# A fused MLP forward and backward on one core: the first pair in half-height products, w1's left-over rows loaded in three pieces, two early pairs in q's banks, all four orders rewritten

## The chip, the cores and the metric

The kernel runs on one core of a Trainium2 chip. The engines are TensorE (PE, with PEld for its weight loads), VectorE (DVE), ScalarE (ACT), GpSimd (POOL) and SyncE (SP, which here only issues transfers). The metric is the time of one execution on the device in microseconds. The kernel before takes 266.25 us, the median of three runs (266.03 to 266.30); the execution that was profiled took 265.99 us, of which the profile covers a span of 264.2 us.

## The reference

A two-layer MLP with GELU, and all its gradients. S is 2048 rows, D is 448, F is 1792, everything is bf16.

```
def _fwd_reference(x, w1, b1, w2, b2):
    h = jnp.einsum("bsd,df->bsf", x, w1) + b1
    h = _gelu(h)                                  # tanh form
    return jnp.einsum("bsf,fd->bsd", h, w2) + b2

_out, _vjp = jax.vjp(_f, x, w1, b1, w2, b2)
return (_out, *_vjp(grad_out))                    # out, gx, gw1, gb1, gw2, gb2
```

## The kernel before, in words

**Tiling.** The 2048 rows are four blocks b of 512. The 1792 columns of F are 14 tiles of 128, taken as 7 pairs per block, so there are 28 pairs p (p = 7b + pair). For each pair the kernel computes u = x w1 (512 rows by two tiles), q = grad_out w2^T, h = gelu(u) and gh = q gelu'(u). From h comes out (units `o`), from gh comes gx (units `x`). At the end, over all rows, come gw1 (line 755) and gw2 (line 809), each 224 or more products of full height.

**Half-height products.** D is 448 = 3 x 128 + 64 rows of contraction. `uq_run` (line 245) cuts all of it into pieces of 64 rows and lets two products of 64 rows run side by side, one on the upper and one on the lower half of the array. One u or q of a pair is a run `.1` of three such double slots, which starts both banks, and a run `.2` of four, which ends them; seven slots of 512 columns. Between the two runs the halves change banks. `run` (line 224) therefore puts a GpSimd instruction between them (`nc.gpsimd.nop`, line 233) when nothing else guarantees that the first run has ended: TensorE's first product of the second run waits for GpSimd, and GpSimd for the end of the first run. In the orders another run nearly always stands in between.

Run `.2` reads a second copy of w1's first 64 rows, on partitions 64 to 127, shifted by one column (`w1f` pieces of the load; "repeated rows"); both runs read w1's last 64 rows ("left-over rows", `w1r`). Before the change the very first pair is computed otherwise: in two halves of 256 columns (tokens `h0`, `h1`), each by `full_run` (line 275), with products of 128 rows for k = 0 to 2 and of 64 rows for k = 3.

**Orders.** Nothing is scheduled by a tool. `Plan` holds one list of operations per engine, in the order of the strings PE_ORDER, ACT_ORDER, DVE_ORDER and SP_ORDER (lines 91 to 132); each engine's queue is strictly in order, and semaphores between engines follow from who writes and reads what. The tokens that matter:

- PE: `h0.1` is half 0 of pair 0, run 1 (before the change `h0.0` is all of half 0); `u5.2` and `q5.2` are run 2 of pair 5; `p1.0` to `p1.3` are the out units of pair 1 of block 0, two slots each; `o1.0.4.9.1` and `x...` are out and gx units (block, half of the rows, first and last tile, run).
- ACT and DVE: `c5A`, `c5B` copy u out of its two banks with the bias; `s`, `g`, `t` are Square, GELU and Tanh on ACT; `e r y z m n` are the derivative's steps on DVE; `G5` multiplies by q and frees q's banks.
- SP: `L0` to `L4` are parts of w1's first 384 rows, `R` its left-over rows and (before) `R2`, `R3` the repeated rows; `K0` to `K3` parts of w2; `X1`, `Y0` transposed blocks of x and grad_out; `J0` to `J3` parts of w2 transposed, `I0`, `I1` halves of w1 transposed, `E` four small copies (`ends`); then `So`, `Sx` stores, `H` stores of h, `T` transposes of gh.

q of pairs 0, 1, 2 and 3, and 4 to 6 of each block need J0, J1, J2 and J3 (`W2_PART`, line 306); `p` units of the same pairs need K0 to K3.

**Banks.** PSUM has eight banks. q lives in banks 6 and 7; u in 4 and 5, but for the pairs in `U_BANK` (line 134); the out and gx units in 0 to 3.

**Semaphores of transfers.** The transfers of SP and ACT share eight semaphores in turn; the order listing shows each transfer waiting for the one eight before it.

Of the kernel before, what the change touches and what calls it, by code (L numbers as in the profile page):

```python
# [96 lines left out]
x0.1.0.6.1 q9.1 u16.1 q9.2 u16.2 x0.0.0.6.2 q10.1 u17.1 q10.2 u17.2 x0.1.0.6.2 q11.1 x0.0.6.10.1 u18.1 q11.2 u18.2
x0.1.6.10.1 x0.0.6.10.2 x0.1.6.10.2 u19.1 q12.1 u19.2 q12.2 x0.0.10.14.1 u20.1 x0.1.10.14.1 u20.2 x0.0.10.14.2
x0.1.10.14.2 q13.1 o2.0.0.6.1 q13.2 o2.1.0.6.1 o2.0.0.6.2 o2.1.0.6.2 q14.1 o2.0.6.10.1 q14.2 o2.1.6.10.1 o2.0.6.10.2
q15.1 u21.1 q15.2 u21.2 o2.1.6.10.2 o2.0.10.14.1 o2.1.10.14.1 u22.1 q16.1 u22.2 q16.2 o2.0.10.14.2 u23.1 o2.1.10.14.2  # L100
u23.2 q17.1 x1.0.0.6.1 x1.1.0.6.1 q17.2 x1.0.0.6.2 x1.1.0.6.2 x1.0.6.10.1 x1.1.6.10.1 q18.1 x1.0.6.10.2 u24.1 q18.2
# [17 lines left out]
c7B r3 y3 z3 G1 m3 e4 n3 r4 y4 z4 G2 e5 r5 m4 z5 vo0.2 vo0.3 vo0.0 vo0.1 G3 y5 n4 e6 r6 y6 z6 G4 m5 e7 n5 r7 y7 m6 z7
G5 n6 e8 r8 m7 z8 y8 n7 G6 e9 r9 y9 z9 m8 n8 m9 G7 vo1.0 vo1.1 vo1.2 vo1.3 n9 e10 r10 y10 z10 G8 m10 e11 n10 r11 y11  # L120
z11 G9 m11 e12 n11 r12 y12 z12 G10 m12 e13 n12 r13 y13 z13 G11 m13 e14 n13 r14 y14 z14 m14 n14 G12 e15 r15 y15 z15
vx0.0 vx0.2 G13 m15 e16 n15 r16 y16 z16 m16 G14 n16 e17 r17 y17 z17 G15 m17 e18 n17 r18 y18 z18 m18 n18 G16 vo2.0
vo2.1 vo2.2 vo2.3 e19 r19 y19 z19 m19 G17 n19 e20 r20 y20 z20 m20 n20 G18 e21 r21 y21 z21 vx1.0 G19 e22 vx1.3 m21 r22
# [35 lines left out]
def make_plan(tc, ctx, x, w1, b1, w2, b2, grad_out, out_0, out_1, out_2, out_3, out_4, out_5):  # L159
    nc = tc.nc  # L160
    P = 128
# [113 lines left out]
    def full_run(w, t, banks, pair, c0, c1):  # L275

        two = []
        for i in (0, 1):
            ft = 2 * (pair % NPB) + i
            for k in range(4):  # L280
                rows = slice(0, 128) if k < 3 else slice(0, 64)
                two.append((k == 3, i, k, lambda i=i, k=k, ft=ft, rows=rows: nc.tensor.matmul(  # L282
                    bk_(banks[i])[:, 0:c1 - c0], lhsT=w[rows, k, ft * P:(ft + 1) * P], rhs=t[rows, k, EDGE + c0:EDGE + c1],
                    start=(k == 0), stop=(k == 3), skip_group_check=True)))
        for _, _, _, product in sorted(two, key=lambda m: m[:3]):
            product()

# [111 lines left out]
    def C(p, h, eng, hf=None):  # L399
        ft = 2 * (p % NPB) + h  # L400
        v = val(("ub", p), F_UB[p])
        if hf is None:
# [4 lines left out]
        bias = b1T[:, ft:ft + 1]
        if eng == "ACT":
            fn = lambda: nc.scalar.activation(out=out, in_=src, func=ACT.Identity, bias=bias)  # L409
# [177 lines left out]
    def LW1R(part, eng="SP"):  # L587

        c0, c1 = ((0, 1024), (1024, F))[part % 2]
        if part < 2:  # L590
            dma(eng, f"w1r{part}", w1_sb[0:64, 3, c0:c1], w1[MAIN:D, c0:c1], [], [("w1r", part)], (c1 - c0) * 128)
        else:
            dma(eng, f"w1f{part - 2}", w1_sb[64:128, 3, c0:c1], w1[0:64, c0:c1], [], [("w1f", part - 2)], (c1 - c0) * 128)
# [259 lines left out]
```

## Time and profile before

| | |
|---|---|
| median of three runs | 266.25 us (266.03 to 266.30) |
| profiled execution | 265.99 us, span 264.2 us |
| PE busy | 260.4 us, 99% of the span |
| DVE, ACT, POOL busy | 198.9, 130.6, 14.1 us |
| forward and gradient units (line 238) | from 7.5 us to 176.6 us |
| gw1 (line 755), gw2 (line 809) | 42.5 us each, to the end |
| mean DMA traffic | 175 GB/s |

An engine's busy time counts from the start of an instruction to its modelled end; PE's products overlap, so its 99% means that there is always one under way, not that the array is full. In a timeline each row is a start, a length, the engine, the source line, the operation with the tiles that it writes and reads, the number of instructions that were merged into the row, and in brackets the idle time before it with what ended it. SPq rows are transfers being issued: their length is the time that SP spends on the issue, not that of the transfer.

### The profile page before, as it was taken

Reading aid. Unit: us, or ns where it says so; the run is one execution under the profiler, and the core shown is the slowest. Engines: PE = TensorE matmul, PEld = TensorE weight load, DVE = VectorE, ACT = ScalarE, POOL = GpSimd, SP = SyncE. Lnnn points to the kernel's source line nnn. Section 1 sums busy time; section 2 is a strip of 40 time slices with the busy share of each in tenths; the row PEclk is TensorE's granted clock in tenths of the full one; section 3 lists DMA queues with packets and bytes.
Section 4 is the critical chain, followed back from the end, with each engine's and each line's share of the span. In section 5 each row is a group of like instructions: output and inputs, shape, how many; then the busy total and the mean of one; then the engine's idle time right before and its main releaser. Section 6 shows DMA issues by size and latency. Waiting matters only on the chain.

```text
span 264.2 us, 5339 instructions
## 1 busy us (share of the span) xinstructions
PE 260.4 (99%) x2170; PEld 182.7 (69%) x2170; DVE 198.9 (75%) x289; ACT 130.6 (49%) x168; POOL 14.1 (5%) x8
## 2 busy tenths in 40 slices
PE   8999999999999999999999999999999999999995
PEld 4488988888888886677777777765555555555554
DVE  6887998999998789897876998339999999311000
ACT  4899786996998936736696511011112111000001
POOL 0000000000000000000000000000000393400000
PEclk9999999999999999999999999999999999999999
DMA  7999689999999953393665934794799988984221
GB/s 199 278 189 257 118 174 189 333 243 257 229 219 197 231 139 66 87 223 85 74 173 160 291 99 104 132 309 108 164 228 158 168 218 171 244 157 130 69 72 35
DMA packets 120235, 46.10 MB, mean 175 GB/s; under 512 B 96671, under 2 KB 120081, under 8 KB 120210
## 3 DMA queue, kind: packets, MB, share of 16 engines
q1 hardware_dynamic: 119636, 45.43, 76.6%
q8 instruction: 17, 0.28, 0.4%
q10 hardware_dynamic: 574, 0.33, 0.4%
q14 instruction: 8, 0.07, 0.1%
HBM read 7.70 MB, written 14.28 MB: 83 GB/s over the span
## 4 chain that ended last, share of the span: by engine, by line
PE 97%; ACT 1%; DVE 1%; issue 0%; ACTq 0%; DVEq 0%
PE bank L238 46%; PE bank L755 16%; PE bank L809 16%; PE qb L238 16%; PE qb L365 1%; ACT TR L427 1%; PE bank L282 1%; PE bank L564 1%; DVE ub L411 0%; ACT ub L409 0%; DVE TR L432 0%; DVE TR L437 0%; PE qb L630 0%; ACT w_sb L814 0%; ACTq L427 0%
## 5 line engine op out<-in xcount | busy, mean ns | idle before, releaser
L238 PEld LDWEIGHTS <-HG 64*128 64x128 bf16 x896 | 70.9, 94 | 17.8 <-issue 0.7
L238 PE MATMUL qb<-gT,w2Tf 64*128 64x512 bf16 x392 | 55.9, 376 | 0.0
L238 PE MATMUL bank<-xT,w1f 64*128 64x512 bf16 x378 | 53.4, 376 | 0.0
L238 PE MATMUL bank<-w_sb,HG 64*128 64x448 bf16 x448 | 51.2, 349 | 0.4 <-ACT ub L409 0.4
L238 PE MATMUL bank<-w1T_sb,HG 64*128 64x448 bf16 x448 | 48.4, 349 | 0.0
L809 PE MATMUL bank<-w2Tf,HG 128*128 128x448 bf16 (+2 forms) x240 | 42.6, 340 | 0.0
L755 PE MATMUL bank<-w1f,gh_nat 128*128 128x448 bf16 x224 | 42.5, 352 | 0.0
L467 DVE SCALAR_TENSOR_TENSOR HG<-TR,qb 128x1024 bf16<-128x1024 bf16 x28 | 34.1, 1217 | 9.6 <-PE qb L238 9.4
L238 PEld LDWEIGHTS <-w2Tf 64*128 64x128 bf16 x392 | 32.6, 94 | 8.2 <-issue 0.2
L238 PEld LDWEIGHTS <-w1f 64*128 64x128 bf16 x378 | 31.4, 94 | 8.3 <-issue 0.3
L809 PEld LDWEIGHTS <-HG 128*128 128x128 bf16 x240 | 22.9, 98 | 19.8
L755 PEld LDWEIGHTS <-gh_nat 128*128 128x128 bf16 x224 | 21.8, 98 | 20.6 <-issue 0.4
L452 ACT ACTIVATE TR<-TR 128x1024 bf16<-128x1024 bf16 x28 | 29.3, 1050 | 11.3 <-DVE TR L442 11.3
L778 DVE TENSOR_TENSOR w1T_sb<-w1T_sb,gh_nat 128x1792 f32<-128x1792 f32 x14 | 28.4, 2025 | 0.5
L457 DVE TENSOR_SCALAR TR<-TR 128x2048 bf16<-128x2048 bf16 x28 | 19.3, 689 | 8.3 <-ACT TR L452 8.3
L760 ACT ACTIVATE TR<-bank 128x448 bf16<-128x448 f32 x14 | 7.6, 543 | 34.9 <-PE bank L755 34.9
L815 DVE CAST w_sb<-bank 128x448 bf16<-128x448 f32 x6 | 3.7, 624 | 25.9 <-PE bank L809 25.9
L814 ACT CAST w_sb<-bank 128x448 bf16<-128x448 f32 (+2 forms) x9 | 4.4, 490 | 37.7 <-PE bank L809 37.7
L784 POOL PARTITION_ALL_REDUCE w1T_sb<-w1T_sb x1 | 10.7, 10662 | 208.3 <-DVE w1T_sb L782 208.3
L409 ACT ACTIVATE ub<-bank,b1T 128x512 bf16<-128x512 f32 (+1 forms) x26 | 16.2, 666 | 10.9 <-DVE TR L442 6.0
L462 DVE TENSOR_TENSOR TR<-TR 128x1024 bf16<-128x1024 bf16 x28 | 19.2, 686 | 0.2
L447 DVE TENSOR_TENSOR TR<-TR,HG 128x1024 bf16<-128x1024 bf16 x28 | 19.2, 684 | 0.0
(45 smaller groups left out, 183.6 us busy)
## 6 DMA issues: line engine op xcount, KB each, us to landing
hT_dram<-HG SPq DMA_DIRECT2D x28, 256.0 KB, 3.4
out_dram<-st SPq DMA_DIRECT2D x16, 224.0 KB, 2.7
w1f<-in_x_dram SPq DMA_DIRECT2D x2, 896.0 KB
w2Tf<-in_grad_out_dram SPq DMA_DIRECT2D x2, 560.0 KB
out_dram<-w_sb SPq DMA_DIRECT2D x2, 448.0 KB, 2.7
out_dram<-xT SPq DMA_DIRECT2D x2, 384.0 KB, 3.1
w_sb<-in_w_dram SPq DMA_DIRECT2D x1, 672.0 KB
w2Tf<-in_grad_out_dram SPq DMA_DIRECT2D x1, 672.0 KB, 4.6
```

The costliest lines, as they stand in the source:

```text
L238: m = nc.tensor.matmul(bk_(b)[:, 0:n], lhsT=l, rhs=r, start=st, stop=sp, skip_group_check=True)
L409: fn = lambda: nc.scalar.activation(out=out, in_=src, func=ACT.Identity, bias=bias)
L447: pl.op("DVE", f"R{p}", lambda: nc.vector.tensor_tensor(out=t[:, 1], in0=t[:, 1], in1=hblk(p), op=ALU.mult), [("r", p), ("h", p)], [val((" ...
L452: pl.op("ACT", f"t{p}", lambda: nc.scalar.activation(out=t[:, 0], in_=t[:, 0], func=ACT.Tanh), [("y", p)], [val(("t", p), ("TR0", p % NTR) ...
L457: pl.op("DVE", f"m{p}", lambda: nc.vector.tensor_scalar(out=t[:], in0=t[:], scalar1=1.0, scalar2=None, op0=ALU.subtract), [("t", p), ("r2" ...
L462: pl.op("DVE", f"n{p}", lambda: nc.vector.tensor_tensor(out=t[:, 0], in0=t[:, 0], in1=t[:, 1], op=ALU.mult), [("m0", p), ("m1", p)], [val( ...
L467: pl.op("DVE", f"G{p}", lambda: nc.vector.scalar_tensor_tensor(out=ghblk(p), in0=t[:, 0], scalar=2.0, in1=qb[:, :, :], op0=ALU.subtract, o ...
L755: nc.tensor.matmul(bk_(bk)[:, 0:D], lhsT=gh_nat[:, st // 4, ft, st % 4, :], rhs=x_nat[:, st, :], start=(st == 0), stop=(st == NS - 1))
L760: fn = (lambda dst=dst, src=src: nc.scalar.mul(out=dst, in_=src, mul=-0.5)) if eng == "ACT" else \
L778: nc.vector.tensor_tensor(out=hs3, in0=a, in1=gh_nat[:, st // 4, :, st % 4, :], op=ALU.add)
L784: pl.op("POOL", "gb1", lambda: nc.gpsimd.partition_all_reduce(gb1_w, hsum, channels=P, reduce_op=bass_isa.ReduceOp.add), ["hsc"], ["gb1"], ...
L809: nc.tensor.matmul(bk_(bk)[:, 0:d1 - d0], lhsT=h_nat[ft][:, st, :], rhs=g_nat[:, st, d0:d1], start=(st == 0), stop=(st == NS - 1))
```

## The change

1. `full_run` is gone. Pair 0's halves are two runs each like every other pair: `h0.1 h0.2 h1.1 ... h1.2`, seven double slots of 256 columns per half.
2. Since `h0.2` needs the repeated rows and the shifted column of x at once, w1's left-over and repeated rows are each loaded in three parts (columns 0 to 256, 256 to 1024, 1024 to 1792) instead of two, six small loads instead of four; the copy of x's edge column (`Dx0`) waits for one quarter of the block only.
3. Pairs 2 and 5 keep u in banks 6 and 7 (before, pair 2 had banks 2 and 3 and pair 5 had 4 and 5). More buffers for u's copies are used (`UB` up to 13).
4. All four orders are new. Out and gx units are cut at tiles 4 and 9 instead of 6 and 10.

On TensorE, where pair 0 begins, there stand before (w1f is w1, xT0 the transposed first block of x):

```order
L282 MATMUL bank4_93<-xT0_68,w1f_64 128x256
L282 LDWEIGHTS w1f_64
L282 MATMUL bank5_94<-xT0_68,w1f_64 128x256
L282 LDWEIGHTS w1f_64
L282 MATMUL bank5_94<-xT0_68,w1f_64 128x256
L282 LDWEIGHTS w1f_64
L282 MATMUL bank5_94<-xT0_68,w1f_64 128x256
L282 LDWEIGHTS w1f_64
L282 MATMUL bank4_93<-xT0_68,w1f_64 128x256
```

and after, at the seam of `h0.1` and `h0.2` (rows of 64 partitions each, two side by side):

```order
L238 MATMUL bank5_94<-xT0_68,w1f_64 128x256
L238 LDWEIGHTS w1f_64
L238 MATMUL bank4_93<-xT0_68,w1f_64 128x256
L238 LDWEIGHTS w1f_64
L238 MATMUL bank4_93<-xT0_68,w1f_64 128x256
L238 LDWEIGHTS w1f_64
L238 MATMUL bank5_94<-xT0_68,w1f_64 128x256
```

The third of these products is the first of `h0.2`; it follows `h0.1` directly and waits for GpSimd.

On SP, the first loads after x's rows, before (64x1024 and 64x768 are left-over and repeated rows, 128x3x256 are L1, L2, L3, 128x3x768 is L4, w2_sb are K0, K1, K2):

```order
L507 DMA w1f_64<-in_w1_dram 64x1024
L507 DMA w1f_64<-in_w1_dram 128x3x256
L507 DMA w1f_64<-in_w1_dram 64x1024
L507 DMA w1f_64<-in_w1_dram 128x3x256 x2
L507 DMA w1f_64<-in_w1_dram 64x768
L507 DMA w2_sb_66<-in_w2_dram 128x2x448
L507 DMA w1f_64<-in_w1_dram 128x3x768
L507 DMA w2_sb_66<-in_w2_dram 128x2x448
L507 DMA w1f_64<-in_w1_dram 64x768
L507 DMA w2_sb_66<-in_w2_dram 128x4x448
```

and after:

```order
L499 DMA w1f_64<-in_w1_dram 64x256 x2
L499 DMA w1f_64<-in_w1_dram 128x3x256
L499 DMA w1f_64<-in_w1_dram 64x768 x3
L499 DMA w1f_64<-in_w1_dram 128x3x256 x2
L499 DMA w2_sb_66<-in_w2_dram 128x2x448
L499 DMA w1f_64<-in_w1_dram 128x3x768
L499 DMA w1f_64<-in_w1_dram 64x768
L499 DMA w2_sb_66<-in_w2_dram 128x6x448
L499 DMA w2_sb_66<-in_w2_dram 128x4x448
L499 DMA w2_sb_66<-in_w2_dram 128x2x448
```

L2 has moved from the fourth to the seventh place, and K3 (6x448) has come forward into this list, ahead of K2 and K1.

On SP, the transposes that follow, before (w2Tf in the order J0, J1, J2, J3 with the tail of J3 from `ends`; w1T_sb are I0 and I1, gT1 is Y1):

```order
L519 DMA_TRANSPOSE gT0_70<-in_grad_out_dram 128x4x512
L519 DMA_TRANSPOSE xT1_69<-in_x_dram 128x4x544
L519 DMA_TRANSPOSE w2Tf_65<-in_w2_dram 128x4x256
L507 DMA w2_sb_66<-in_w2_dram 128x6x448
L519 DMA_TRANSPOSE w2Tf_65<-in_w2_dram 128x4x256
L519 DMA_TRANSPOSE w2Tf_65<-in_w2_dram 128x4x512
L507 DMA ends_72<-in_x_dram 16x448
L507 DMA ends_72<-in_grad_out_dram 16x448
L507 DMA ends_72<-in_w2_dram 16x448 x2
L519 DMA_TRANSPOSE w2Tf_65<-in_w2_dram 128x4x752
L521 DMA_TRANSPOSE w2Tf_65<-ends_72 128x4x16
L510 DMA_TRANSPOSE w1T_sb_67<-in_w1_dram 128x7x448 x2
```

and after:

```order
L511 DMA_TRANSPOSE xT1_69<-in_x_dram 128x4x544
L511 DMA_TRANSPOSE gT0_70<-in_grad_out_dram 128x4x512
L511 DMA_TRANSPOSE w2Tf_65<-in_w2_dram 128x4x256
L511 DMA_TRANSPOSE w2Tf_65<-in_w2_dram 128x4x512
L511 DMA_TRANSPOSE w2Tf_65<-in_w2_dram 128x4x256
L502 DMA_TRANSPOSE w1T_sb_67<-in_w1_dram 128x7x448
L511 DMA_TRANSPOSE gT1_71<-in_grad_out_dram 128x4x544
L502 DMA_TRANSPOSE w1T_sb_67<-in_w1_dram 128x7x448
L499 DMA ends_72<-in_x_dram 16x448
L499 DMA ends_72<-in_grad_out_dram 16x448
L499 DMA ends_72<-in_w2_dram 16x448 x2
L511 DMA_TRANSPOSE w2Tf_65<-in_w2_dram 128x4x752
```

I0, Y1 and I1 now stand ahead of `E` and J3 (the 752 columns).

The diff, with a line or two of each order:

```diff
 PE_ORDER = """
-W7 X0 X1 X2 X3 B h0.0 h1.0 u1.1 u2.1 u1.2 u3.1 u2.2 u3.2 p0.0 p0.1 u4.1 p0.2 p0.3 u4.2 p1.0 p1.1 p1.2 u5.1 p1.3 p2.0
+W7 X0 X1 X2 X3 B h0.1 h0.2 h1.1 u1.1 h1.2 u2.1 u1.2 u3.1 u2.2 u3.2 p0.0 p0.1 p0.2 p0.3 u4.1 u5.1 u4.2 u5.2 p1.0 p1.1
...
-u8.2 q2.1 p5.2 p5.3 q2.2 u9.1 p6.0 p6.1 u9.2 q3.1 p6.2 p6.3 q3.2 u10.1 o1.1.0.6.1 u10.2 q4.1 o1.0.0.6.1 u11.1 q4.2
+p5.0 p5.1 q1.2 u9.1 p5.2 p5.3 u9.2 q2.1 p6.0 p6.1 q2.2 u10.1 p6.2 p6.3 u10.2 q3.1 o1.1.0.4.1 q3.2 u11.1 o1.0.0.4.1
+u11.2 q4.1 o1.0.0.4.2 q4.2 u12.1 o1.1.0.4.2 u12.2 q5.1 o1.0.4.9.1 u13.1 q5.2 u13.2 o1.1.4.9.1 o1.0.4.9.2 q6.1
...
 SP_ORDER = """
-xr12 xr24 R0 L1 R2 L2 L3 R1 K0 L4 K1 R3 K2 Y0 X1 J0 K3 J1 J2 E J3 I0 I1 Y1 X2 So0.1 H0 H1 H2 H3 H4 H5 H6 H7 H8 T0 T1
+xr12 xr24 R0 F0 L1 R1 F1 R2 L2 L3 K0 L4 F2 K3 K2 K1 X1 Y0 J0 J2 J1 I0 Y1 I1 E J3 X2 So0.1 So0.0 H0 H1 H2 H3 H4 H5 H6
...
-UB = (0, 1, 2, 3, 4, 5, 6, 7, 8, 9, 0, 1, 2, 3, 4, 5, 6, 7, 8, 9, 0, 1, 2, 0, 1, 2, 0, 1)
-U_BANK = {1: 0, 2: 2}
+UB = (0, 1, 2, 3, 4, 5, 6, 7, 8, 9, 10, 11, 12, 13, 0, 1, 2, 3, 4, 5, 6, 0, 1, 2, 0, 1, 2, 0)
+U_BANK = {1: 0, 2: 6, 5: 6}
...
-    def full_run(w, t, banks, pair, c0, c1):
...
+    REST = (0, 1, 1, 1, 2, 2, 2)
+    REST_COLS = ((0, 256), (256, 1024), (1024, F))
...
-        rd = [part_w1(p), ("w1r", int(p % NPB > 3))] + [("xT", b, h) for h in hs]
-        if d == 0:
-            pe(f"u{p}.{d}{tag}", lambda: full_run(w1_sb, xT[b % 2], bk, p, *c), rd, vs, ("s256", 8), (None, 0))
-            return
+        rd = [part_w1(p), ("w1r", REST[p % NPB])] + [("xT", b, h) for h in hs]
         if d == 2:
-            rd += [("xe", b), ("w1f", int(p % NPB > 3))]
+            rd += [("xe", b), ("w1f", REST[p % NPB])]
...
-              [(tag, 0, 0)], [v], ("tiny", 1))
+              [(tag, 0, 0) if tag == "gT" else "row0"], [v], ("tiny", 1))
...
+    def LW1F(part, eng="SP"):
+
+        c0, c1 = REST_COLS[part]
+        dma(eng, f"w1f{part}", w1_sb[64:128, 3, c0:c1], w1[0:64, c0:c1], [], [("w1f", part)], (c1 - c0) * 128)
```

More of the change, by code (lines that the diff above doesn't have):

```diff
@@ L97 @@
[L97 to L101, printed above, removed]
@@ L119 @@
[L119 to L123, printed above, removed]
@@ L124 @@
-y22 z22 n21 G20 m22 e23 n22 r23 y23 z23 m23 n23 G21 e24 r24 y24 z24 m24 G22 n24 e25 vx2.2 r25 vx2.3 z25 y25 G23 m25
-e26 n25 r26 y26 z26 m26 G24 n26 e27 r27 y27 z27 G25 m27 vo3.0 vo3.1 n27 vo3.2 vo3.3 G26 G27 vx3.1 vx3.3
+ident X0 Dx0 X2 b1T b2c c0B0 c0B1 c1B e0 r0 y0 c2B c3B z0 e1 r1 y1 z1 c4B e2 c5B r2 y2 z2 c6B m0 n0 Dg0 c7B m1 n1 G0 m2 e3
+n2 r3 y3 z3 G1 e4 r4 m3 z4 n3 y4 G2 vo0.2 vo0.3 m4 vo0.0 vo0.1 n4 G3 e5 e6 r5 r6 z5 z6 y5 y6 G4 m5 m6 n5 n6 e7 r7 y7
+z7 G5 e8 r8 y8 z8 m7 n7 G6 m8 e9 n8 r9 y9 vo1.0 vo1.1 z9 vo1.2 m9 vo1.3 n9 G7 e10 r10 y10 z10 m10 G8 n10 e11 r11 y11
@@ L273, in unit_run @@
         run(slots)
-    def full_run(w, t, banks, pair, c0, c1):
[L277 to L286, printed above, removed]
     def gap(bank):
@@ L411, in C, with after @@
             fn = lambda: nc.vector.tensor_scalar(out=out, in0=src, scalar1=bias, scalar2=None, op0=ALU.add)
-        pl.op(eng, f"c{p}{'AB'[h]}{'' if hf is None else hf}", fn, [uv, "b1T"], [v], ("copy", 512 if hf is None else 256))
+        o = pl.op(eng, f"c{p}{'AB'[h]}{'' if hf is None else hf}", fn, [uv, "b1T"], [v], ("copy", 512 if hf is None else 256))
+        if hf is None and u_banks(p)[0] == 6 and eng == "ACT" and f"c{p}B" in DVE_ORDER.split():
+            after(o, [("u", p, 1)])
+    def after(o, vs):
+        o["after"] = vs
+        return o
     def hblk(p):
@@ L571, in XC @@
         fn = (lambda: nc.scalar.copy(out=out, in_=src)) if eng == "ACT" else (lambda: nc.vector.tensor_copy(out=out, in_=src))
-        pl.op(eng, f"xc{t}", fn, [("xt", t)], [val(("xT", 0, t // 2), ("xT", 0, t // 2))], ("copy", 512))
+        pl.op(eng, f"xc{t}", fn, [("xt", t)], [val(("xT", 0, t // 2), ("xT", 0, t // 2))] + (["row0"] if t == 0 else []), ("copy", 512))
     def LX(src, dst, tag, b, hs):
@@ L587, in LW1R @@
     def LW1R(part, eng="SP"):
[L589 to L593, printed above, removed]
+        c0, c1 = REST_COLS[part]
+        dma(eng, f"w1r{part}", w1_sb[0:64, 3, c0:c1], w1[MAIN:D, c0:c1], [], [("w1r", part)], (c1 - c0) * 128)
+    def LW1F(part, eng="SP"):
+        c0, c1 = REST_COLS[part]
+        dma(eng, f"w1f{part}", w1_sb[64:128, 3, c0:c1], w1[0:64, c0:c1], [], [("w1f", part)], (c1 - c0) * 128)
     def LW2(part, eng="SP"):
@@ L712, in make_plan @@
         elif t == "Nx":
-            rows_nat("xn", x_nat, x2, [("w1", i) for i in range(len(W1_COLS))] + [("w1r", 0), ("w1r", 1), ("w1f", 0), ("w1f", 1)])
+            rows_nat("xn", x_nat, x2, [("w1", i) for i in range(len(W1_COLS))] + [(v, i) for v in ("w1r", "w1f") for i in range(3)])
         elif t == "Ng":
```

57 lines of the change are left out of this document (31 added, 26 removed).

## The prediction

> **What bounds the kernel now.** I read the page's head first, then the chain, then the waits of TensorE, then SP's queue in time.
>
> ```profile
> span 264.2 us, 5339 instructions
> PE 260.4 (99%) x2170; PEld 182.7 (69%) x2170; DVE 198.9 (75%) x289; ACT 130.6 (49%) x168; POOL 14.1 (5%) x8
> PE 97%; ACT 1%; DVE 1%; issue 0%; ACTq 0%; DVEq 0%
> PE bank L238 <- ACT ub L409: 0.4, 1, 0.4
> ```
>
> PE is under way for 260.4 of 264.2 us, 97% of the chain that ended last is PE, and the last row (waits) is the only wait on another compute engine that it shows once real products run. So two things alone can move the end: fewer or shorter products, and a new wait of PE. Nothing behind could absorb a new wait, because PE never stands still later; waits at several places do not add, though: the place where PE is latest against the kernel before decides.
>
> PE's rows that give the prices (pieces of PE's timeline; the last three of the chain in time):
>
> ```profile
> 5.66 2.12 PE L282 MATMUL bank<-xT,w1f 128*128 128x256 bf16 x15
> 7.73 0.38 PE L238 MATMUL bank<-xT,w1f 64*128 64x512 bf16 x2
> 12.99 1.05 PE L238 MATMUL bank<-w_sb,HG 64*128 64x448 bf16 x8 [0.39 <-ACT ub L409]
> 13.79 0.90 PE L238 MATMUL bank<-xT,w1f 64*128 64x512 bf16 x6
> 22.86 0.91 PE L238 MATMUL qb<-gT,w2Tf 64*128 64x512 bf16 x6
> 41.38 0.91 PE L238 MATMUL qb<-gT,w2Tf 64*128 64x512 bf16 x6
> 23.12 0.65 PE qb L238 x6
> 23.77 0.76 PE bank L238 x8
> 24.52 0.86 PE qb L238 x8
> ```
>
> They are pair 0 (from 5.66), the second slot of pair 1 (7.73; its first began with the row above), the first out unit `p0.0` (12.99), `u4.1` (13.79), `q0.1` (22.86) and `q4.1` (41.38). The chain's rows say what runs cost when nothing waits: a `.1` run 0.65 us for three double slots, a `.2` run 0.86 for four, so 0.216 a slot of 512 columns and 1.51 a pair; four slots of 448 columns 0.76, so 0.19 each.
>
> **The opening on PE.** Before, pair 0 takes 2.07 us (5.66 to 7.73). After, it is 14 double slots of 256 columns, half of 0.216 each: 1.51 us. Added is the seam between `h0.1` and `h0.2`: PE ends, GpSimd sees it, PE's next weights wait for GpSimd. No run of the kernel before follows its own first half directly, so this is bounded.
>
> ```profile
> PEld L238 <- POOLq L233: 0.3, 2, 0.2
> ```
>
> Two such waits of weight loads cost 0.3 us in all, that is about 0.15 each where other products covered most of it; zero is the lower end. The upper end is one product's full length, 0.38 (row at 7.73), after which nothing of the first run is left. I take 0.25. Pair 0 then costs 1.76, a gain of 0.31.
>
> From 5.66 to `p0.0` at 12.99 are 7.33 us, of which pair 0 and pairs 1 to 3 are 2.07 + 3 x 1.51 = 6.60. So 0.73 us were waits (0.39 shows as idle, the rest lies under the modelled ends): `p0.0` needs the bank from which pair 2's u has just been copied. With pair 2 in q's banks that wait has no cause any more. Without any new wait `p0.0` would come at 5.66 + 1.76 + 4.53 = 11.95, a gain of 1.04.
>
> **The loads that this needs.**
>
> ```profile
> SPq L507 <- DMA TR<-in_x_dram: 0.8, 1, 0.8
> 3.69 0.48 SPq L507 DMA_DIRECT2D w1f<-in_w_dram  x1
> 4.21 0.59 SPq L507 DMA_DIRECT2D w1f<-in_w_dram  x1
> 6.07 0.59 SPq L507 DMA_DIRECT2D w_sb<-in_w_dram  x1
> TR<-in_x_dram SPq DMA_DIRECT2D x1, 128.0 KB, 2.8
> w1f<-in_w_dram SPq DMA_DIRECT2D x1, 192.0 KB, 3.8
> 7.74 0.48 SPq L507 DMA_DIRECT2D w1f<-in_w_dram  x1
> w1f<-in_w_dram SPq DMA_DIRECT2D x1, 576.0 KB, 6.3
> ```
>
> The first row is SP standing still for 0.8 us until x's first rows have landed: the ninth transfer waits for the first, since eight semaphores go round. Its end is the issue at 3.69. After the change the ninth is L1, and L2 is the thirteenth, in the place of K0, which was issued at 6.07; before, L2 went out at 4.21. The rows with KB give the time from issue to landing: 2.8 us for the first load in an empty queue, 3.8 for L2 itself in a full one, 6.3 for L4. L2 thus lands between 8.9 and 9.9. `u2.1` is reached at 5.66 + 1.76 + 0.65 (`u1.1`) = 8.07 and waits 0.8 to 1.8 us. I take 1.1, nearer to the empty queue, because the two small loads ahead of it carry 32 KB where 128 KB went. That eats the 1.04: by `p0.0` the opening is even, with a gain of 0.2 and a loss of 0.8 as its ends.
>
> L4 is issued where R3 was (row at 7.74) and took 6.3 us; with 14.0 it is there before `u4.1`, which now has `p0.2` and `p0.3` ahead of it (13.79 + 0.76 = 14.55). c2, c3 and the GELUs keep their engines and prices; since two pairs' banks are now free longer, I cost the moves on ACT and DVE at nothing. Their cover: q of every early pair has 1.51 + 0.76 = 2.27 us more PE work ahead of it (`u7`, `p3.2`, `p3.3` before `q0.1`), so each G has that much longer. If it is gone, the G before a q holds PE.
>
> **The transposes, and the term that decides.** SP's queue in time, then landings and the transfers' share by stretch:
>
> ```profile
> 8.26 1.00 SPq L507 DMA_DIRECT2D w_sb<-in_w_dram  x1
> 9.30 5.68 SPq L519 DMA_TRANSPOSE gT<-in_grad_out_dram  x1
> 15.03 3.13 SPq L519 DMA_TRANSPOSE xT<-in_x_dram  x1
> 18.20 1.30 SPq L519 DMA_TRANSPOSE w2Tf<-in_w_dram  x1
> 20.19 4.86 SPq L519 DMA_TRANSPOSE w2Tf<-in_w_dram  x2
> 25.09 0.60 SPq L507 DMA_DIRECT2D ends<-in_x_dram  x1
> 26.36 2.24 SPq L507 DMA_DIRECT2D ends<-in_w_dram  x2
> 28.64 2.99 SPq L519 DMA_TRANSPOSE w2Tf<-in_w_dram  x1
> 32.94 7.58 SPq L510 DMA_TRANSPOSE w1T_sb<-in_w_dram  x2
> 40.56 3.09 SPq L519 DMA_TRANSPOSE gT<-in_grad_out_dram  x1
> w2Tf<-in_w_dram SPq DMA_TRANSPOSE x1, 3.7
> w2Tf<-in_w_dram SPq DMA_TRANSPOSE x1, 5.5
> w_sb<-in_w_dram SPq DMA_DIRECT2D x1, 672.0 KB
> 9.00:13.50 4.50, 4.11 (x39) 2.16 (x37) 3.81 (x8) 4.35 (x7) 0.00 (x0) 1.00 1.13 294
> 21.00:24.30 3.30, 3.30 (x36) 3.02 (x34) 2.84 (x5) 3.29 (x5) 0.00 (x0) 1.00 1.09 287
> 27.10:30.20 3.10, 3.10 (x34) 2.77 (x30) 3.10 (x7) 2.60 (x4) 0.00 (x0) 1.00 0.12 20
> ```
>
> The timeline's rows are Y0, X1, J0, J1 with J2, `ends`, J3, I0 with I1, and Y1. SP is held for microseconds by each transpose; Y0 took 5.68 us while the plain loads drained (DMA share 1.13 from 9.0 to 13.5), X1 of nearly the same size 3.13. The landing rows are J0 (issued 18.20) and J3 (issued 28.64), 3.7 and 5.5 us; the row with 672 KB is K3. Before, J3 lands at 28.64 + 5.5 = 34.1 and `q4.1` needs it at 41.38: 7 us to spare.
>
> After, I0, Y1 and I1 stand ahead of `ends` and J3. Everything up to the end of J1 and J2 is the same set of transfers as before, whose issue ended at 20.19 + 4.86 = 25.05; three more plain loads are now issued ahead of the transposes and one (K3, 672 KB or 0.69 MB, 2.4 us at the 287 GB/s of its stretch) less among them. So that end stays where it was, or moves by up to 1.5 us (2.1 for the three, less 0.6): I take 0.7, so 25.75. Then I0, I1 and Y1: 7.58 + 3.09 and small gaps, 36.55. Then `ends`, from 25.09 to 28.60 before, 3.51; if one of the four pieces need not wait, 4 x 0.6 = 2.4; I take 2.95, so 39.5. Then J3: 5.5 to its landing and the gap, 45.05. The lower end (no lag, quick `ends`) is 43.8, the upper (1.5 lag, 3.51) 46.4. Below the lower end it goes only if J3 flows behind I1 without SP's pause for `ends`, in which the DMA engines stood nearly idle before (0.12, last row): some 1 us less, 42.9.
>
> When does PE want it? The work ahead of `q4.1` is that of before plus `u11` (1.51) and two more slots of out units (0.38): 41.38 + 1.89 = 43.27 for a kernel that is even up to there, as I have it. PE then waits 45.1 - 43.3 = 1.8 us. Behind `q4.1` stands all the rest of PE's list; G4, and through it `q5`, and the copies of u12 and u13 start as much later. Nothing gives it back.
>
> Of the gates between, J0 (`q0.1`) is the nearest: with K3's 2.4 us moved ahead of it, it lands at 18.20 + 3.7 + 2.4 + 0.7 = 25.0, and `q0.1` wants it at 22.86 + 2.27 = 25.13. DVE's edge copy of grad_out now waits for Y0 behind X1; `c7B`, `m1` and `G0` stand behind it, and `q1.1` behind G0 has the 2.27 us. Both end before J3's lateness and do not add to it. gw1 and gw2 at the end keep their instructions and their order.
>
> The sum: profiled execution 265.99 (span 264.2 and 1.79 around it) + 1.8 = 267.8; the median of the runs lies 0.26 above that execution: 268.1 us.
>
> **The clock.** At the start PE ran at half rate:
>
> ```profile
> 0.76 3.14 PE L365 MATMUL qb<-const-bfloat16-1.0 128*128 128x512 bf16 x7 [0.76 <-PEq L837]
> ```
>
> 3.14 / 7 = 0.45 us per 512 columns against 0.216 later. The Trainium skill (TensorE: Matmul & The Clock Gate, "Part 1: The HAM clock gate (the "warmup" mystery)") says that the array's clock falls back to half after an idle window of about 3.4 us. By that rule a wait of 1.8 us leaves the clock alone, and one at the late end of J3 comes near it; the kernel before has no such pause to show it.
>
> **Rivals.** *J3 in time, opening won* (faster). The transposes run without holding SP, J3 lands before 42.5, and L2 by 8.3. Then the 1.04 of the opening less a little wait remains: about 265.5. For it: X1 and Y1, out of the rush, took 3.1 where Y0 took 5.68, and J3's 7 us to spare. Against: I0, I1, Y1 already are priced out of the rush and alone take 10.7 us. It decides where J3 lands before about 42.7. *J3 just in time, opening even* (same): 266.3; needs J3 by 43.8, the lower end of the sum. *PE waits long enough for half rate*: if J3 slips to its upper end or beyond, PE pauses 3.1 us or more, and may begin again as it began at the start, where it ran at half rate from 0.76 until pair 0 at 5.66, some 4 us of work; that loses half of it, 2 us: 266.25 + 3.1 + 2 = 271.4. *That pair 0's new form alone counts* (loads and transposes all covered, `p0.0` still waiting for another copy): 266.25 - 0.31 = 265.9.
>
> **Numbers.** J3 late, main case, 0.69, with its ends 43.8 and 46.4: 266.8 to 269.4. J3 just in time 0.13. J3 in time and opening won 0.10. Pair 0's form alone 0.04. Half rate 0.04. A change below 0.2% (0.5 us) cannot be told from none, since the runs spread over 0.27. Faster by more than that: 0.10, and 0.02 of the just-in-time case where the opening gains, 0.12. Within: the other 0.11 of that case and the 0.04 of pair 0's form, 0.15. Slower: 0.69 and 0.04, 0.73. For 8 in 10 the range leaves out the half rate and the lowest openings: 265.6 to 269.7.
>
> **What would show it.** PE idle before a product `qb<-gT,w2Tf` near 43 to 45 us, ended by a DMA into w2Tf, of 1 to 3 us: right. An idle of PE at 8 to 9.5 us ended by a DMA into w1f, and none any more before the first `w_sb,HG` product: the opening as priced. SP's J3 issued at 39 to 40 us. The prediction is wrong if J3 is issued by 37, or if PE stands still at another place for longer.

## The result, and the profile after

The changed kernel takes 268.95 us, the median of five runs (267.73 to 269.79), against 266.1 us of the kernel before on the same chip (265.83 to 266.3): a ratio of 1.0102, with an interval of 1.0068 to 1.0135. It is slower by 2.85 us. The execution that was profiled is the quickest of the five, 267.73 us.

The head of its page and its chain, then its waits of PE and of PE's weight loads (in total, times, longest):

```profile
span 265.9 us, 5349 instructions
PE 260.3 (98%) x2182; PEld 144.3 (54%) x2182; DVE 195.1 (73%) x281; ACT 134.6 (51%) x176; POOL 14.1 (5%) x8
PE 82%; SPq 13%; DMA 3%; issue 0%; ACTq 0%; ACT 0%
```

```profile
PE bank L238 <- DMA w_sb<-in_w_dram: 1.0, 1, 1.0
PE qb L238 <- DVE ub L397: 0.7, 1, 0.7
PE qb L238 <- DMA w2Tf<-in_w_dram: 0.3, 1, 0.3
PEld L238 <- POOLq L233: 1.1, 5, 0.4
PEld L238 <- DMA w1f<-in_w_dram: 0.9, 1, 0.9
PEld L238 <- DMA w2Tf<-in_w_dram: 0.8, 1, 0.8
```

PE's work is as long as before (260.3 against 260.4 us), and the span grew by 1.7 us. The chain was 97% PE; now the first 45 us of it run over SP's queue and a transfer (16%). Where PE stood still, its timeline shows in brackets:

```profile
5.83 2.64 PE L238 MATMUL bank<-xT,w1f 64*128 64x256 bf16 x34
9.14 0.82 PE L238 MATMUL qb<-xT,w1f 64*128 64x512 bf16 x6 [0.66 <-DVE ub L397]
13.03 1.68 PE L238 MATMUL bank<-w_sb,HG 64*128 64x448 bf16 x16
18.70 0.93 PE L238 MATMUL bank<-w_sb,HG 64*128 64x448 bf16 x8 [0.96 <-DMA w_sb<-in_w_dram]
26.26 0.83 PE L238 MATMUL qb<-gT,w2Tf 64*128 64x512 bf16 x6
44.90 0.82 PE L238 MATMUL qb<-gT,w2Tf 64*128 64x512 bf16 x6 [0.32 <-DMA w2Tf<-in_w_dram]
```

These are pair 0 with `u1.1`, then `u2.1`, `p0.0`, `p1.0`, `q0.1` and `q4.1`. To tell how late PE is at a place, its start in the kernel before is taken and the work added that now stands ahead. `p0.0` is even (13.03 against 12.99). `p1.0` waits for K1 and is 1.14 us late: the kernel before has it at 16.05, and `u5` (1.51) is added ahead of it, which makes 17.56. Its row there, which the prediction does not show:

```profile
16.05 1.39 PE L238 MATMUL bank<-w_sb,HG 64*128 64x448 bf16 x12
```

`q0.1` is still late by as much, 26.26 against 25.13. `q4.1` is 1.63 us late, 44.90 against 43.27, and nothing is added behind it. So the three waits that the view shows do not add: the 0.32 before `q4.1`, counted from the modelled end of the product ahead, is only what J3 costs beyond the lateness that K1 had already caused. The wait before `u2.1` is put down to a copy on DVE; the weight load of `u2.1` has its own row among the waits (0.9 for w1f), L2 landed at 9.09 and that copy ended at 9.11. In a second trace of this kernel, below, the same wait (0.90 us, `u2.1` at 9.05) is put down to w1f, so L2 is what it waits for.

SP's queue in time (X1, Y0, then J0, J2 and J1, I0, Y1, I1, the four pieces of `ends`, J3), and the chain's piece behind it:

```profile
11.61 6.81 SPq L511 DMA_TRANSPOSE xT<-in_x_dram  x1
18.47 2.31 SPq L511 DMA_TRANSPOSE gT<-in_grad_out_dram  x1
20.82 5.37 SPq L511 DMA_TRANSPOSE w2Tf<-in_w_dram  x3
26.24 4.45 SPq L502 DMA_TRANSPOSE w1T_sb<-in_w_dram  x1
30.73 2.35 SPq L511 DMA_TRANSPOSE gT<-in_grad_out_dram  x1
33.12 3.97 SPq L502 DMA_TRANSPOSE w1T_sb<-in_w_dram  x1
37.14 0.59 SPq L499 DMA_DIRECT2D ends<-in_x_dram  x1
37.77 0.58 SPq L499 DMA_DIRECT2D ends<-in_grad_out_dram  x1
38.40 1.22 SPq L499 DMA_DIRECT2D ends<-in_w_dram  x2
39.66 3.17 SPq L511 DMA_TRANSPOSE w2Tf<-in_w_dram  x1
39.66 5.20 DMA w2Tf<-in_w_dram
```

J3 is issued at 39.66 and lands at 44.86; `q4.1` starts 0.04 us later.

### The profile page after: what moved, and what is told of

It reads as the page before. It is cut to its first block, busy times and chain, and to the rows that moved or that the text cites. A ratio compares the mean times of both kernels' runs of the same rounds, so it can differ in the third digit from the quotient of the medians.

```text
span 265.9 us, 5349 instructions
## 1 busy us (share of the span) xinstructions
PE 260.3 (98%) x2182; PEld 144.3 (54%) x2182; DVE 195.1 (73%) x281; ACT 134.6 (51%) x176; POOL 14.1 (5%) x8
## 4 chain that ended last, share of the span: by engine, by line
PE 82%; SPq 13%; DMA 3%; issue 0%; ACTq 0%; ACT 0%
PE bank L238 36%; PE bank L745 16%; PE bank L799 16%; PE qb L238 14%; SPq L511 6%; SPq L499 3%; SPq L502 3%; DMA w2Tf<-in_w_dram 2%; DMA w1f<-in_w_dram 1%; ACTq L499 0%; ACT w_sb L804 0%
## 5 line engine op out<-in xcount | busy, mean ns | idle before, releaser
L238 PEld LDWEIGHTS <-HG 64*128 64x128 bf16 x896 | 52.4, 94 | 36.7 <-issue 1.5
L238 PE MATMUL qb<-gT,w2Tf 64*128 64x512 bf16 x392 | 52.5, 376 | 0.3 <-DMA w2Tf<-in_w_dram 0.3
L238 PE MATMUL bank<-w_sb,HG 64*128 64x448 bf16 x448 | 48.8, 349 | 1.0 <-DMA w_sb<-in_w_dram 1.0
L238 PE MATMUL bank<-xT,w1f 64*128 64x512 bf16 (+1 forms) x378 | 48.2, 368 | 0.1
L238 PE MATMUL bank<-w1T_sb,HG 64*128 64x448 bf16 x448 | 47.2, 349 | 0.0
L238 PEld LDWEIGHTS <-w1f 64*128 64x128 bf16 x406 | 22.1, 94 | 19.8 <-DMA w1f<-in_w_dram 0.9
L238 PEld LDWEIGHTS <-w2Tf 64*128 64x128 bf16 x392 | 22.5, 94 | 18.6 <-DMA w2Tf<-in_w_dram 0.8
L395 ACT ACTIVATE ub<-bank,b1T 128x512 bf16<-128x512 f32 (+1 forms) x23 | 14.4, 665 | 11.2 <-PE bank L238 9.8
```

Of the source, the lines that this page charges most:

```text
L238: m = nc.tensor.matmul(bk_(b)[:, 0:n], lhsT=l, rhs=r, start=st, stop=sp, skip_group_check=True)
```

## The experiments

The theory: the loss is J3's landing behind I0, Y1 and I1, with K1's landing hidden in it, and what the products of pair 0 gain does not show. Rivals: one of the two waits alone carries it; or the new lists of PE, ACT and DVE, or pair 0's form, cost something.

**The changed kernel again.**

> The changed kernel itself once more, on the same chip as the run before it. Theory (its time hangs on when J3 lands, which differs from run to run by a microsecond or more): median 268 to 269.3 us with a spread of 1 to 2 us, and in the profiled run the same three places, u2.1, p1.0 and q4.1, at which PE waits for a transfer, q4.1 right behind J3's landing. Rival (the first profile showed a chance case): another place, or no wait before q4.1.

268.48 us (267.77 to 269.38), 1.0086 [1.0068, 1.0104]. This time the profiled execution is the longest of its batch, 269.38 us with a span of 267.6. Its timeline at `p1.0` and `q4.1`, then the last of `ends` and J3 in its chain:

```profile
18.71 0.93 PE L238 MATMUL bank<-w_sb,HG 64*128 64x448 bf16 x8 [1.06 <-DMA w_sb<-in_w_dram]
46.56 0.82 PE L238 MATMUL qb<-gT,w2Tf 64*128 64x512 bf16 x5 [1.96 <-DMA w2Tf<-in_w_dram]
39.85 1.49 SPq L499
41.38 5.13 DMA w2Tf<-in_w_dram
```

`p1.0` is where it was (18.71 against 18.70). J3 was issued 1.72 us later and landed at 46.51 instead of 44.86, 1.65 later, and the execution is 1.65 us longer (269.38 against 267.73). Between these two runs the whole difference is that of one transfer's landing. Of the 1.72 on SP, 0.4 had come up before I0 (issued at 26.65 instead of 26.24), 0.4 more on I0, Y1 and I1, and 0.9 on the last piece of `ends`, 1.49 long where it was 0.59.

**J3 ahead of I0, Y1 and I1; K1 ahead of K3; both.** The first:

```diff
-J2 J1 I0 Y1 I1 E J3 X2
+J2 J1 E J3 I0 Y1 I1 X2
```

> The changed kernel with one move on SP: the four ends copies and J3 go ahead of I0, Y1 and I1; all else as changed. Theory (the latest gate decides; J3 is the latest): J3 lands near 34 us, PE no longer waits for it at q4.1, and what is left is the lateness that PE already had at p1.0 (18.70 where the kernel before would stand at 16.05 + 1.51 = 17.56, 1.1 us): 266.1 + 1.1 = 267.2 us. Rival (J3's wait was only the 0.3 us of idle that the waits list shows): 0.3 us below the changed kernel, 268.6. Rival (something else, run by run, makes the spread of 267.7 to 269.8): median stays at 268.9.

267.12 us (266.75 to 267.36), 1.0031 [1.0019, 1.0043]. What its waits of PE still show, and `q4.1`:

```profile
PE bank L238 <- DMA w_sb<-in_w_dram: 1.2, 1, 1.2
PE qb L238 <- DVE ub L397: 0.7, 1, 0.7
44.52 0.84 PE L238 MATMUL qb<-gT,w2Tf 64*128 64x512 bf16 x6
```

J3 lands at 35.16 and is not waited for; these five runs spread over 0.6 us, those of the changed kernel over 2.1. What remains is K1: `q4.1` at 44.52, 1.25 late.

```diff
-L4 F2 K3 K2 K1 X1
+L4 F2 K1 K2 K3 X1
```

> The changed kernel with one move on SP: w2's parts go in the order K1, K2, K3 instead of K3, K2, K1. Theory (the latest gate decides): the wait of 0.96 us at p1.0 for K1 goes, but PE then waits longer at q4.1 for J3, which lands as before at 44.9; the end does not move, 268.9 us against 268.95. Rival (waits add up): about 1.0 us less, 267.9.

269.43 us (268.25 to 271.01), 1.0119 [1.0094, 1.0144]: K1 in time alone gains nothing. The longest of the six had a mean granted clock of 0.994 (1 is TensorE's full clock), the others 0.998 to 1.000. PE reaches `q0.1` and `q4.1` earlier and waits there:

```profile
25.86 0.82 PE L238 MATMUL qb<-gT,w2Tf 64*128 64x512 bf16 x6 [0.59 <-DMA w2Tf<-in_w_dram]
45.85 0.82 PE L238 MATMUL qb<-gT,w2Tf 64*128 64x512 bf16 x6 [1.68 <-DMA w2Tf<-in_w_dram]
```

Both edits together:

> The changed kernel with both moves: ends and J3 ahead of I0, Y1, I1, and K1, K2, K3 in that order. Theory: both late gates are gone; left are the first product of pair 2 waiting for L2 (PE at p0.0 then stands where it stood before, 13.0 us) and J1 at q1.1, which landed at 29.9 where PE would want it at 29.7: 266.1 + 0.2 = 266.3 us, with a spread as small as before's. Rival (the new orders on the compute engines cost by themselves): stays above 267.5.

266.77 us (266.22 to 267.53), 1.0016 [1.0006, 1.0027], so 2.2 of the 2.85 us are back. It is not quite even, and 0.5 us above what was expected, since J0 now gates:

```profile
25.99 0.82 PE L238 MATMUL qb<-gT,w2Tf 64*128 64x512 bf16 x6 [0.84 <-DMA w2Tf<-in_w_dram]
```

J0 landed at 25.95 with K3's 672 KB ahead of it, 0.82 behind the 25.13 at which `q0.1` wants it. Three gates stand one behind the other, each hidden by the one before or behind it: K1 at `p1.0` (1.1 us), J0 at `q0.1` (0.8), J3 at `q4.1` (1.6 and more).

**J3 late in the kernel before.** The one move of SP's list that the prediction rested on, without the rest of the change:

```diff
-J1 J2 E J3 I0 I1 Y1 X2
+J1 J2 I0 Y1 I1 E J3 X2
```

> The kernel before with one move on SP: I0, Y1 and I1 go ahead of the ends copies and J3, as in the change; nothing else. Theory: J3's issue then starts at 25.05 + 7.58 + 3.09 + 0.1 + 3.5 = 39.3 and lands 5.5 later at 44.8, q4.1 stood at 41.38, so the time is 266.1 + 3.4 = 269.5 us. With quick ends copies (2.4 us) 268.4. Rival (transposes are taken up by the queue faster when nothing else is late): under 267.

271.24 us (270.63 to 272.99), 1.0188 [1.0174, 1.0201]: the move alone costs more than the whole change, since here `q4.1` comes 1.89 us of work earlier. It also costs 1.7 us more than was expected, and the trace shows why. The profiled execution took 272.99 us. Its `q4.1`, two stretches behind it (sum, busy PE, PEld, DVE, ACT, POOL, then the granted clock, DMA share, GB/s), and behind them `q5.1` in this kernel and in the kernel before:

```profile
45.63 1.46 PE L238 MATMUL qb<-gT,w2Tf 64*128 64x512 bf16 x6 [3.94 <-DMA w2Tf<-in_w_dram]
45.63:52.00 6.37, 6.37 (x34) 2.39 (x36) 0.00 (x0) 0.10 (x1) 0.00 (x0) 0.54 0.95 263
45.63:56.00 10.37, 10.37 (x74) 4.23 (x76) 3.98 (x7) 3.22 (x6) 0.00 (x0) 0.72 0.97 290
53.81 0.81 PE L238 MATMUL qb<-gT,w2Tf 64*128 64x512 bf16 x6
```

```profile
46.67 0.91 PE L238 MATMUL qb<-gT,w2Tf 64*128 64x512 bf16 x6
```

After a pause of 3.94 us PE works at a granted clock of 0.54: from `q4.1` to `q5.1` it takes 53.81 - 45.63 = 8.18 us, against 46.67 - 41.38 = 5.29 before, 2.89 us lost beside the pause. This is the half-rate rival's mechanism, on the far side of its condition. Pauses of up to 2.16 us in the traces of the other runs left the clock at 1.00. The Trainium skill (TensorE: Matmul & The Clock Gate, "Part 1: The HAM clock gate") has half rate set in after an idle window of about 3.4 us and calls the window free-running. The runs agree: the six mean clocks of this kernel are 1.000, four times 0.994 and 0.987, so that, by an estimate, 0.6 or 1.3% of some 270 us, 1.6 or 3.5 us, went to the clock or not, run by run. The four runs at 0.994 took 271.10 to 271.41; less 1.6 us that is the expected 269.5 or little more. The run at 1.000 took 270.63, 4.3 us above the kernel before, so it seems to have stood still for about as long and kept its clock: the length of a pause alone does not settle whether half rate follows.

**Pair 0's form alone.** The new form, its six small loads and the early edge copy, with all other orders, banks and cuts of the kernel before:

```diff
-B h0.0 h1.0 u1.1
+B h0.1 h1.1 h0.2 h1.2 u1.1
-R0 L1 R2 L2 L3 R1 K0 L4 K1 R3 K2 Y0
+R0 F0 L1 R1 L2 F1 L3 K0 L4 R2 K1 F2 K2 Y0
```

> The kernel before with pair 0's new form alone: the halves as runs of double slots (h0.1, h1.1, h0.2, h1.2, u1.1), the left-over and repeated rows in three parts each, the edge copy behind one quarter; all other orders, banks, buffers and cuts as before. Theory (pair 0 costs 1.51 instead of 2.07 us): pair 0 and u1.1 0.3 to 0.56 us shorter, and p0.0, which still waits for a copy of pair 2, takes back some of it: 265.8 to 266.1 us. Rival (the wait before p0.0 is set by the chain of copies on DVE and ACT, which begins as early as the loads allow): all of it is taken back there, 266.2 to 266.4, with the idle time before p0.0 longer by as much as pair 0 is shorter.

266.75 us (266.1 to 267.7), 1.0007 [0.9981, 1.0033]: no gain that can be told. Its opening:

```profile
5.30 2.54 PE L238 MATMUL bank<-xT,w1f 64*128 64x256 bf16 x34
8.46 4.06 PE L238 MATMUL bank<-xT,w1f 64*128 64x512 bf16 x36 [0.62 <-DMA w1f<-in_w_dram]
12.74 1.05 PE L238 MATMUL bank<-w_sb,HG 64*128 64x448 bf16 x8 [0.22 <-ACT ub L395]
13.83 0.88 PE L238 MATMUL bank<-xT,w1f 64*128 64x512 bf16 x6
```

Pair 0 is done earlier, and then PE waits 0.62 us for L2 (landed 8.42), 0.22 for the copy before `p0.0`, and 0.33 for L4 at `u4.1` (12.74 and four slots of 0.19 make 13.50; L4 landed at 13.79). The kernel before has `u4.1` at 13.79. So a shorter pair 0 is worth nothing by itself: the loads take it back at the next three places. There is a fourth place, `p4.0`; its row here, the chain's piece ahead of it, and its row in the kernel before:

```profile
26.49 0.93 PE L238 MATMUL bank<-w_sb,HG 64*128 64x448 bf16 x8 [0.36 <-DMA w_sb<-in_w_dram]
20.64 5.81 DMA w_sb<-in_w_dram
```

```profile
25.78 1.02 PE L238 MATMUL bank<-w_sb,HG 64*128 64x448 bf16 x8
```

With six small loads instead of four, SP issues K3 1.09 us later than before (20.64 against 19.55), it lands at 26.45, and `p4.0` is 0.71 us late; this profiled execution is 0.82 us longer (266.81 against 265.99). So the edit changes the loads as well as the products, and the 266.75 is no price of the products alone. The rival is right that all of the gain is taken back, but neither its time (266.2 to 266.4) nor its mechanism (a longer wait before `p0.0`, which is 0.22 us here and was 0.39) came out.

**The best list for SP.** The changed kernel with all four gates moved (L2 two places earlier, K1 ahead, K3 back behind J0, J3 ahead):

```diff
-R0 F0 L1 R1 F1 R2 L2 L3 K0 L4 F2 K3 K2 K1 X1 Y0 J0 J2 J1 I0 Y1 I1 E J3 X2
+R0 F0 L1 R1 L2 F1 L3 K0 L4 R2 F2 K1 K2 X1 Y0 J0 K3 J1 J2 E J3 I0 Y1 I1 X2
```

> The changed kernel with SP's list alone written anew: L2 fifth instead of seventh, K1 and K2 right behind F2, K3 back behind J0, E and J3 ahead of I0, Y1, I1. Theory (all that was lost by the change lies in the order of SP's list: L2, K1, J0 and J3 each late by 0.7 to 1.7 us, one behind the other; pair 0's form and the moves on PE, ACT and DVE lose nothing): L2 lands near 8.0, J0 near 23.5, J3 near 34; no wait of PE before u2.1, p1.0, q0.1 or q4.1; the opening's gain stays, less a wait for L4 where it lands behind 14.0 (up to 0.5 us): 265.3 to 265.9 us. Rival (the new lists of PE, ACT and DVE or the other cut of the units cost something that the late loads hide): 266.3 or more although none of the four loads is waited for.

267.04 us (266.43 to 269.3), 1.0038 [1.0015, 1.006]. With the seam covered as well:

```diff
-B h0.1 h0.2 h1.1 u1.1 h1.2 u2.1
+B h0.1 h1.1 h0.2 u1.1 h1.2 u2.1
```

> As the run before it, and on PE h1.1 stands between h0.1 and h0.2, and u1.1 between h0.2 and h1.2, so that no second run follows its own first half. Theory (the seam costs 0.28 us of PE, as the trace of the changed kernel has it): pair 0 and u1.1 take 0.28 us less, u2.1 is reached as much earlier and, if L2 is there, 0.0 to 0.3 us less than the run before it; the full 0.28 if nothing else in the opening is waited for. Rival (the next load, L2 or L4, takes the place of the seam): equal within 0.1 us, and the wait before u2.1, p0.0 or u4.1 longer by the 0.28.

266.62 us (265.65 to 269.81), 1.001 [0.9991, 1.003]. And the same list but with the changed kernel's first loads, L2 late, and the seam as it is:

```diff
-L4 F2 K3 K2 K1 X1 Y0 J0 J2 J1 I0 Y1 I1 E J3 X2
+L4 F2 K1 K2 X1 Y0 J0 K3 J1 J2 E J3 I0 Y1 I1 X2
```

> The changed kernel's first loads as they are (L2 seventh), but K1, K2 ahead of X1, K3 back behind J0, and E and J3 ahead of I0, Y1, I1. Theory: K1 and J0 and J3 are in time (J0 near 23.5 against 25.13), so that only the opening is left, which the wait for L2 at u2.1 (0.7 us) and the seam make even with the kernel before or 0.2 to 0.4 us better: 265.9 to 266.3 us. Beside the run with L2 early it shows L2's share: 0.3 to 0.7 us. Rival (K3's 672 KB ahead of J0 is not what makes J0 late): q0.1 still waits 0.5 us or more for w2Tf and the time stays near 266.8.

266.9 us (266.25 to 268.39), 1.0018 [1.0001, 1.0036]. The four gates are open, but both theories missed a fifth. Rows of the kernel with the best list, of the one without the seam, and of the one with L2 late:

```profile
26.27 0.93 PE L238 MATMUL bank<-w_sb,HG 64*128 64x448 bf16 x8 [0.71 <-DMA w_sb<-in_w_dram]
```

```profile
27.45 0.93 PE L238 MATMUL bank<-w_sb,HG 64*128 64x448 bf16 x8 [2.16 <-DMA w_sb<-in_w_dram]
44.94 0.83 PE L238 MATMUL qb<-gT,w2Tf 64*128 64x512 bf16 x6
```

```profile
9.25 0.82 PE L238 MATMUL qb<-xT,w1f 64*128 64x512 bf16 x6 [1.06 <-DMA w1f<-in_w_dram]
43.42 0.83 PE L238 MATMUL qb<-gT,w2Tf 64*128 64x512 bf16 x6
```

The rows with a wait for w_sb are `p4.0`, which waits for K3 where K3 stands behind J0 (landed 26.2 and 27.4, wanted near 25.4); by the new order of PE it stands ahead of `q0.2`. That is why the changed kernel had brought K3 forward, and what it cost was K1 and J0. The row at 9.25 is `u2.1` with L2 late. That kernel reaches `q4.1` at 43.42, almost even; the one without the seam at 44.94, or 42.78 if its 2.16 are taken off. The 0.64 between them is what L2's place and the seam cost together, by one trace each.

**K3 covered.** In the kernel without the seam, `p4.0` to `p4.3` now stand behind `u8.2`:

```diff
-u7.2 p3.3 q0.1 p4.0 p4.1 q0.2 u8.1 p4.2 p4.3 u8.2 q1.1
+u7.2 q0.1 p3.3 u8.1 q0.2 u8.2 p4.0 p4.1 p4.2 p4.3 q1.1
```

> As the run without the seam and with SP's best list, and on PE the units p4.0 to p4.3 stand behind u8.2 (u7.2, q0.1, p3.3, u8.1, q0.2, u8.2, p4.0 ...), so that K3 is wanted near 27.5 instead of 25.4 us, while it landed at 26.2 to 27.4 in the runs with K3 behind J0. Theory (what was left over in those runs was the wait of p4.0 for K3, 0.7 to 2.2 us, and nothing else): no wait for w_sb any more, q4.1 near 42.8, and 266.6 less 0.7 to 1.0: 265.6 to 265.9 us, faster than the kernel before by 0.1 to 0.25%, and the spread of the runs below 0.8 us. Rival (the transfers as a whole are late, and the next one, J0 at q0.1 or J1 at q1.1, takes K3's place): 266.2 to 266.6, with a wait of PE before a product of gT and w2Tf.

265.87 us (265.59 to 266.33), 0.9989 [0.998, 0.9998], and the spread is down to 0.74 us. PE's products wait for no transfer any more (its weight loads still wait 0.7 us for w1f); the only wait for a compute engine is that of `u8.1`, for ACT's copy of pair 7:

```profile
25.45 0.80 PE L238 MATMUL bank<-xT,w1f 64*128 64x512 bf16 x5 [0.32 <-ACT gh_nat L395]
42.84 0.91 PE L238 MATMUL qb<-gT,w2Tf 64*128 64x512 bf16 x6
```

So that copy goes ahead of a Square on ACT:

```diff
-t0 g6 t1 s3 c7A t2
+t0 g6 t1 c7A s3 t2
```

> As the run with K3 covered, and on ACT the copy c7A stands ahead of the Square s3. Theory (there PE stood still only for 0.32 us before u8.1, since ACT copied pair 7's u behind s3): the wait is gone, q4.1 comes near 42.5, 265.4 to 265.7 us, faster than the kernel before by 0.2 to 0.3%. Rival (ACT is full, so s3 and with it G3 or a GELU come late elsewhere): 265.8 to 266.2, with a new wait of PE on ACT or DVE within the next 15 us.

265.59 us (265.41 to 266.18), 0.9972 [0.9957, 0.9988]: faster than the kernel before by 0.28%, and than the changed one by about 3 us. PE's products have no wait left but one before pair 0, and `q4.1` comes 0.58 us ahead of the even 43.27:

```profile
42.69 0.83 PE L238 MATMUL qb<-gT,w2Tf 64*128 64x512 bf16 x6
```

So pair 0's form, the banks for pairs 2 and 5 and the new lists of DVE and nearly all of ACT's and PE's lose nothing. What the change lost lies in SP's order and in where PE's list asks for those loads: with SP's list alone written anew the best medians were 266.77 to 267.04, and the rest came with PE's list (the seam covered, `p4.0` to `p4.3` moved).

## Why the prediction was right, and where not

**The direction and the place** came as forecast: slower, by PE waiting before `q4.1` for J3, issued behind I0, Y1 and I1. Moving that alone in the kernel before made it slower by 1.88%, of which some 0.6%, by an estimate from the mean clock of 0.994 of most of its runs, is the clock.

**J3's landing, term by term.** J1 and J2 issued by 25.75: it was 26.19. I0, Y1 and I1 until 36.55: 37.09. `ends` 2.95, until 39.5: 2.48, until 39.62. J3 5.5 to its landing, 45.05: 5.20, 44.86. The single misses, up to 0.5 us, cancel; that the sum hits to 0.1 us is luck. The four pieces of `ends` show it: they took 2.5 us here, but 3.1 to 3.9 in nine of the thirteen traces, 3.4 in the second of this kernel. `q4.1` wanted at 43.27, late by 1.8: 1.63. The sum against the profiled execution, 267.8, measured 267.73.

**The step from the profiled execution to the median** was mis-sized. The prediction added 0.26, what the kernel before has between its profile and its median. But the new end hangs on one landing, at 44.86 in one profile and 46.51 in the other, and the profiled execution was the early one; the median lies 1.22 above it in the first batch. The runs of the changed kernel spread over 1.6 and 2.1 us in the two batches, where three runs of the kernel before had spread over 0.27. J3 is not the only source of spread: with J3 early, in the three kernels with K3 behind J0 and not yet covered, it was 2.1 to 4.2 us, and single runs of the kernel before took up to 269.9. A forecast of 268.1 stands against 268.95 and, in the second batch, 268.48. If every microsecond of the landing is one of the time, as between the two profiles, J3 landed near 46.1 in the median run (44.86 + 1.22, an estimate), between the value taken and its upper end, 46.4.

**The opening** came out even, as taken (13.03 against 12.99). The seam was taken as 0.25: the first product of `h0.2` came 0.38 us behind the one ahead of it, where 0.11 is the usual distance, so 0.27. Pair 0 and `u1.1` took 2.48 us (1.76 + 0.65 = 2.41 was the sum), by the starts of single products. L2 landed at 9.09, taken as 9.2. The wait before `p0.0` is gone. Covering the seam with `h1.1` gave back less than its price: with K3 covered, pair 0 and `u1.1` still took 2.33, since `h1.1` then stands 0.11 us behind its turn, right after ACT's copy of x's second half (ended at 6.18, `h1.1` at 6.23).

**What was missed** is a gate: K1. The step "what this needs" priced L2, L4, J0 and J3, but not K1, which now stands last behind K3 and K2 (672 and 448 KB) and lands at 18.66 where `p1.0` wants it at 17.56. It did not change the time, because J3 is later still and lateness at one place covers lateness at another. It would have ended the *just in time* rival: with J3 early, K1 alone left the kernel 0.31% slower. J0's landing, taken as 25.0 against 25.13, was 25.02; it showed as a wait only once K1 had been put right. The moves on ACT, costed at nothing, held 0.32 us at `u8.1`, which showed only once the loads were in time.

**The rivals.** *Pair 0's form alone*, 265.9, showed no gain: 266.75, with the loads as the reason, K3 among them. The interval, 0.9981 to 1.0033, does not rule out the 0.13% that was forecast, but the trace shows no such gain. *Half rate* is a real mechanism, shown in the kernel before with J3 late; in the changed kernel the pause was 0.32 and 1.96 us in the two traces, and the mean clock of all eleven runs 0.999 or 1.000. The start of the kernel, from which the prediction took it, is weaker evidence: there the products are 0.45 us long, but the granted clock that the profile gives for that stretch is 1.00. Its price was taken as 2 us and measured as 2.89 in one trace. *J3 in time, opening won*, 265.5, is nearly what the last kernel reaches, but it needed L2, K1, K3 and the copy on ACT as well.

**Open** is why SP was held 1.49 us instead of 0.59 by the last piece of `ends` in the second trace (in nine of the thirteen traces one of the four pieces, not always the same, took 1.2 to 2.0 us, in the kernel before too), and more generally what moves a landing by a microsecond or more between runs of the same kernel.

## What to carry to other kernels

Where TensorE never rests, write down for each load when it lands and when it is wanted before you reorder a queue, and also for the loads that do not move but get bytes put ahead of them: here five of them (L2, K1, K3, J0, J3) were gates in turn, and mending one showed the next. Waits at several places do not add, so undoing one of them alone says little; the place where the kernel is latest decides, and only a run with all of them opened shows what the rest of the change is worth. Where the end hangs on one landing, a single profile may lie at either end of the runs' spread, as the two of the changed kernel did.

## What was not expected of the hardware

A transpose holds SP while the plain loads ahead of it drain, whichever transpose it is: X1 took 3.13 us of SP in the kernel before, behind Y0, and 6.81 us (7.09 in the second trace) when it came first; Y0 took 5.68 there and 2.31 here. The cost belongs to the place in the queue, not to the transfer. It follows the bytes ahead: X1's issue ended at 18.42 with K3's 672 KB ahead of it, and at 16.15 and 16.36 in two kernels with K3 behind J0.

A single pause of PE is not only its own length: one of 3.94 us was followed by half rate, 2.89 us more, while those of 2.16 us and less in the traces were not. What lies between is not measured, and it differs by run: of six runs of one kernel one kept its clock, and in three other kernels whose traces pause 0.71 to 2.16 us (K1 in time, the best list, the best list without the seam) one run each had a mean clock of 0.993 or 0.994 and was the longest of its batch, 269.30 to 271.01 us. How long PE paused in those runs is not on record.
